# Second-layer weights loaded as two neighbouring rows a partition, weight loads thinned out beside the last attention blocks, and routing placements issued later

## The chip, the cores and the metric

The kernel runs on one core of a Trainium2 chip. The metric is the device time of one execution in microseconds. "TensorE" is PE in the profile, "VectorE" DVE, "ScalarE" ACT, "GpSimd" POOL and "SyncE" SP; PEld is TensorE's weight load. The median of three timed runs before the change is 332.24 us.

## The reference

Retention attention over 8 batches, 8 heads, 576 positions and 64 dimensions a head, then a mixture of 8 experts in which each of the 4608 tokens goes to the one expert with the highest logit.

```python
scores = scale * np.matmul(q, k.transpose(0, 1, 3, 2))
ret = scores * Dmat[None, :, :, :]          # gamma_h ** (i - j), causal
x = np.matmul(ret, v)                       # -> x of 4608 x 512
logits = x @ w_gate
expert_idx = np.argmax(logits, axis=1)
...
for e in range(E):                          # 8 experts
    mask = expert_idx == e
    h = np.maximum(x[mask] @ w1[e], 0.0)    # w1[e]: 512 x 1024
    out[mask] = gate_w[mask, None] * (h @ w2[e])   # w2[e]: 1024 x 512
```

## The kernel before

The order of instructions is written out by hand: each engine executes its instructions in the order in which the program issues them, and waits only on data and on buffers.

**Attention.** `blocks` lists 40 blocks, 5 for each of the 8 batches (four of 128 positions, one of 64). The loop over them overlaps stages of neighbouring blocks: transposes, scores, products with values, states. The kernel writes x, in rows, to a DRAM tile `x_rows`, to which a column block `gat` of gate values is added for each batch (SyncE issues both: `put_rows`, `write_gates`). For each finished batch a chain of small VectorE operations (`route_batch`) works out the slot of each token. It contains two products on TensorE: the ranks (`oh` and `incl` with `su1` and `onesb`) and the placements (`pay` with `rh`); `product` issues the next of the two, `steps` the VectorE operations up to it.

**Experts.** When the first five batches are placed, GpSimd gathers rows of `x_rows` by token number (`gather`, tile `xg`, 128 rows each). Each expert has two items: phase 0 with 3 groups of 128 tokens, phase 1 with 2. The list `seq` begins (0,0), (1,0), (0,1), (1,1), (2,0), (2,1), (3,0) and so on; the first number is the expert. For each item `mm1` makes the hidden layer `ht` from the transposed rows `xt` and the first-layer weights `w1b`; `mm2` multiplies it with the second-layer weights `w2b` in 8 chunks `fb` a group, VectorE scales the result by the gate (`ys`), and GpSimd scatters it to `out`. `trans` transposes the rows of the next item between the groups.

**Queues that matter here.** `load_w` loads one part of an expert's weights: four parts of `w1` (128 rows of 1024 values each) and four of `w2` (two chunks of 128 rows of 512 values). The loads turn float32 into bfloat16 and are issued on GpSimd, in one row with its gathers, scatters and tensor operations. `wq` lists the parts by expert: `w1` parts 0 to 3, then `w2` parts 4 to 7. I number the parts of experts 0 and 1 from 0 to 15, so 12 to 15 are expert 1's `w2`. `fetch(n)` issues the next n parts. The dictionary `early` says how many go beside the last attention blocks; one `fetch` follows after the loop; the rest go out in `on`, which is called after each block of `mm1` (8 calls in phase 0, 4 in phase 1) and after each group of `mm2`. The number n in `on` counts these calls: n = 0 to 7 lie in `mm1(0,0)`, 8 to 10 in `mm2(0,0)`, 11 to 18 in `mm1(1,0)`, and 19 to 21 in `mm2(1,0)`. The `script` names what else is done at given n, among it the last placements (`turn`).

PSUM tiles of `mm1` (`pm`) and of the routing products (`pss`) come in turn from one pool of three banks, `psH`, in this stretch: a new tile waits until the third last one has been read.

Of the kernel before, what the change touches and what calls it, by code (L numbers as in the profile page):

```python
# [19 lines left out]
P = 128  # L20
B, H, S, DH = 8, 8, 576, 64
DM = H * DH
E, F = 8, 1024
# [6 lines left out]
NPT = DM // P  # L30
# [7 lines left out]
EW = 2  # L38
# [6 lines left out]
def kernel(  # L45
# [16 lines left out]
    def mm(out, lhsT, rhs, start, stop):  # L62
        nc.tensor.matmul(out=out, lhsT=lhsT, rhs=rhs, start=start, stop=stop, skip_group_check=True)  # L63
# [44 lines left out]
    NB = len(blocks)  # L108
# [48 lines left out]
    for g in range(2):  # L157
        hs = slice(g * NP, (g + 1) * NP)
        nc.sync.dma_start(out=qts[0][:, hs, 0:NCH - 1, :],
                          in_=q[0, hs, P:NCH * P, :].rearrange("h (p s) d -> p h s d", p=P))  # L160
# [103 lines left out]
    def load_w(e, part, n, pool, dep=None):  # L264

        if part == 0:
            wb[e] = (pool.tile([P, NPT, F], BF16, tag="w1", name="w1b"),
                     pool.tile([P, NFB, DM], BF16, tag="w2", name="w2b"))
        m = (NPT, NFB)[part // n] // n
        o = part % n * m  # L270
        w = (moe_w1, moe_w2)[part // n]
        after(nc.gpsimd.dma_start(out=wb[e][part // n][:, o:o + m, :],  # L272
                                  in_=w[e, o * P:(o + m) * P, :].rearrange("(c p) f -> p c f", p=P)), dep)

# [227 lines left out]
    def stage_R(i):  # L504

        if i < 0:
            return
        b, c = blocks[i]
        full = c < NCH
        n, m = (NP, P) if full else (NP // 2, REM)  # L510
        ps = pools["R"](NP)[0:m]
        xb = xbs.pop(i)


        for k in range(n):
            w, a = k // (n // 2), k % (n // 2)
            for u in range(2):
                r = slice(u * DH, (u + 1) * DH)
                o = (ps[r, 2 * a:2 * a + 2, w * DH:(w + 1) * DH] if full
                     else ps[:, 2 * u + w, :].rearrange("p (h d) -> p h d", d=DH))  # L520
                tr(o, xb[:, k * P + u * DH:k * P + (u + 1) * DH], (identb, identx)[w][:, :])
        xr = wk4.tile([P, NP * P], BF16, tag="xr", name="xr")
        t0 = b * S + c * P
        nc.scalar.copy(out=xr[0:m, :].rearrange("p (a t) -> p a t", t=P), in_=ps)  # L524
        todo_x.append((x_rows[t0:t0 + m, 0:DW], xr[0:m, :].bitcast(F32)))
# [3 lines left out]
    def put_rows():  # L529

        while todo_x:
            o, a = todo_x.pop(0)
            nc.sync.dma_start(out=o, in_=a)
# [15 lines left out]
    def stage_L2(b):  # L549
        ps = small()  # L550
        for h in range(2):
            mm(ps[:, h * 32:h * 32 + (32, E)[h]], lt[:, h * P:(h + 1) * P],
               sel[:, NCH * h:NCH + h, :].rearrange("p c n -> p (c n)"), h == 0, h == 1)
        todo_r.append(route_batch(b, ps[:, 0:NCOL * E].rearrange("p (c n) -> p c n", n=E)))
        for _ in range(2):
            next(todo_r[-1])
# [7 lines left out]
    fields, o = {}, 0  # L564
# [216 lines left out]
    def small():  # L781
        return pools["S"]([P, 512], F32)
# [16 lines left out]
    def mm1(e, ph, between):  # L799
        nb = (CA if ph == 0 else CB) // P  # L800
        n = nb * P
        xt = xts.pop((e, ph))
        w1b, w2b = wb[e]
        ht = (hta if ph == 0 else htb).tile([P, NFB, n], BF16, tag="ht", name="ht")
        per = 512 // n
        for f0 in range(0, NFB, per):
            pm = pools["H"]([P, per, n], F32)
            for o in range(per):
                fb = f0 + o
                for c in range(NPT):  # L810
                    mm(pm[:, o, :], w1b[:, c, fb * P:(fb + 1) * P], xt[:, c, :], c == 0, c == NPT - 1)
            nc.scalar.activation(out=ht[:, f0:f0 + per, :], in_=pm[:, :, :], func=AF.Relu)  # L812
            between()
        return ht
# [43 lines left out]
        return [2 * c - 6, 2 * c - 5] if b == 0 and c > 2 else [c - 1] if b > 0 and c > 0 else []  # L858

    wq = [(e, j) for e in range(EW) for j in range(8)] + [(e, j) for e in range(EW, E) for j in range(8)]  # L860
    early = {NB - 7: 1, NB - 6: 2, NB - 5: 2, NB - 4: 1, NB - 3: 1, NB - 2: 1, NB - 1: 2}

    def fetch(n):
        for e, j in [wq.pop(0) for _ in range(min(n, len(wq)))]:
            load_w(e, j, 4, wpool if e < EW else wpool2)
# [65 lines left out]
        if 0 not in slots and len(placed) == BA and c == NCH:  # L931
            make_slots(0)
    gather_first(len(first))
    fetch(len(wq) - 8 * (E - EW))
    pp.close()
    pq = ExitStack()
    psT = pq.enter_context(tc.tile_pool(name="psT", bufs=2, space=PSUM))
# [14 lines left out]
    def turn():  # L952
        product(rf)
        steps(rf, 9)

    script = {0: lambda: stage_L2(B - 1), 1: turn, 2: lambda: (stage_R(NB - 1), put_rows()), 5: turn,
              9: lambda: (turn(), make_slots(1))}
    calls = iter(range(1000))
    last.append(True)
# [1 line left out]
    def on(i):  # L961

        n = next(calls)
        script.get(n, lambda: None)()
        write_gates()
        gather_upto(i + 2)
        if n > 7 and n * 9 % 20 < 9:
            fetch(1)

    seq = ([(e, 0) for e in range(NA)] + [(e, 1) for e in range(NA)]  # L970
# [71 lines left out]
    with tc.If(over > 0):  # L1042
        with ExitStack() as p3:
# [13 lines left out]
            for f in range(2):  # L1057
                src = ev[:, f, :].rearrange("p (b c) -> p b c", c=NCOL)
                dst = nat[f, :].rearrange("(b s) -> b s", s=S)
                for c in range(NCOL):  # L1060
                    n = P if c < NCH else REM
                    w = nc.sync.dma_start(out=dst[:, c * P:c * P + n].rearrange("b p -> p b"), in_=src[0:n, :, c])
# [18 lines left out]
            xt = fb1.tile([P, NPT, P], BF16, name="fxt")  # L1081
            with tc.For_i(0, nr, 1) as t:
# [7 lines left out]
                with tc.For_i(0, E, 1) as e:  # L1090
# [7 lines left out]
                    for f0 in range(0, NFB, 4):  # L1098
                        pm = fps.tile([P, 4, P], F32, name="fpm")
# [45 lines left out]
```

## Time and profile before

| | us |
|---|---|
| median of 3 runs (331.92, 332.24, 336.05) | 332.24 |
| the profiled execution, its own time | 332.26 |
| its span, first to last instruction | 330.4 |
| time outside the span | 1.9 |
| TensorE busy | 310.5 |
| GpSimd busy | 202.5 |

Attention fills the span to about 170 us, the experts the rest. The last TensorE instruction ends near 325 us, and the last scatter's landing closes the span. Idle time of an engine is of interest only where another engine then waits for it.

### The profile page before, as it was taken

The numbers are of one execution on the slowest core, as the hardware profiler recorded it, in microseconds if no ns is written. First come the engines' busy times: TensorE is split into PE (matmuls) and PEld (weight loads), VectorE is DVE, ScalarE is ACT, GpSimd is POOL, SyncE is SP. The second block draws the span as 40 slices with busy tenths as digits, with TensorE's granted clock in tenths as the row PEclk, the third lists the DMA queues.
The fourth block names the chain that finished last, engine by engine and source line by source line (L and its number), as shares of the span: only waits on it lengthen the run. The fifth ranks groups of instructions, "written<-read, shape, count | busy, mean of one in ns | idle before, by whom it ended". The sixth has DMA issues, their size and how long they took to land. (4 is left out here: it accounts for less than half of the span.)

```text
span 330.4 us, 11777 instructions
## 1 busy us (share of the span) xinstructions
PE 310.5 (94%) x4965; PEld 231.7 (70%) x4981; DVE 135.3 (41%) x412; ACT 184.1 (56%) x372; POOL 202.5 (61%) x259
## 2 busy tenths in 40 slices
PE   7999799999999999997888999999999999989993
PEld 5788689888898888887765556656565655646562
DVE  4434256466565646655357622212122313112122
ACT  3469477676777667675565344554545353554530
POOL 4476654635364452554870488888888788888532
PEclk9999999999999999999999999999999999999998
DMA  9999899999998999899799279989999998999921
GB/s 177 229 250 219 183 238 223 233 229 242 247 225 204 223 219 245 199 192 190 127 225 191 77 141 202 217 198 182 216 198 228 206 223 183 188 227 180 263 96 53
DMA packets 118359, 65.96 MB, mean 200 GB/s; under 512 B 89628, under 2 KB 110620, under 8 KB 118304
## 3 DMA queue, kind: packets, MB, share of 16 engines
q0 software_dynamic: 18432, 31.80, 46.1%
q1 hardware_dynamic: 99344, 33.37, 44.6%
q8 instruction: 40, 0.66, 0.9%
q14 instruction: 15, 0.12, 0.1%
q10 hardware_dynamic: 528, 0.02, 0.1%
HBM read 67.45 MB, written 15.53 MB: 251 GB/s over the span
## 5 line engine op out<-in xcount | busy, mean ns | idle before, releaser
L812 ACT ACTIVATE ht<-pm 128x384 bf16<-128x384 f32 (+1 forms) x96 | 50.4, 525 | 57.4 <-PE pm L63 56.6
L308 POOL TENSOR_TENSOR kk<-kt,kg 128x512 f32<-128x512 f32 x39 | 41.4, 1061 | 65.6 <-issue 36.2
L63 PE MATMUL py<-w2b,ht 128*128 128x512 bf16 (+1 forms) x312 | 73.8, 374 | 2.0 <-DMA w2b<-in_moe_w_dram 1.1
L63 PE MATMUL pm<-xt,w1b 128*128 128x384 bf16 (+1 forms) x512 | 72.8, 299 | 0.0
L1005 DVE TENSOR_SCALAR ys<-py,gsl 128x512 f32<-128x512 f32 (+1 forms) x41 | 30.2, 738 | 85.1 <-PE py L63 81.3
L63 PEld LDWEIGHTS <-w1b 128*128 128x128 bf16 x512 | 49.8, 98 | 21.5
L1008 POOL DMA_INDIRECT out_dram<-ys,tids x40 | 41.2, 1031 | 35.3 <-DVE gsl L796 16.2
L433 DVE TENSOR_TENSOR sc<-pssc,mask 128x512 f32<-128x512 f32 x64 | 41.2, 686 | 28.6 <-PE pssc L63 28.6
L63 PEld LDWEIGHTS <-ht 128*128 128x128 bf16 x328 | 30.8, 98 | 31.1 <-issue 1.4
L752 POOL DMA_INDIRECT xg<-x_rows,tidg x40 | 41.2, 1031 | 14.7 <-issue 8.2
L63 PE MATMUL psx<-sc,vt 128*64 128x128 f32 (+1 forms) x640 | 38.4, 265 | 0.4 <-ACT xT L478 0.3
L63 PE MATMUL pssc<-qT,kT 64*64 64x128 f32 (+2 forms) x896 | 36.6, 262 | 0.1
L478 ACT COPY xT<-psx 128x512 f32<-128x512 f32 x32 | 18.7, 586 | 29.8 <-PE psx L63 21.6
L797 ACT COPY xt<-pt 128x512 bf16<-128x512 bf16 x40 | 22.7, 587 | 18.9 <-PE pt L66 18.8
L298 POOL TENSOR_TENSOR qq<-qt,qg 128x512 f32<-128x512 f32 (+1 forms) x28 | 29.4, 1049 | 6.2 <-DMA qt<-in_q_dram 4.3
L366 ACT COPY kT<-pst 128x512 f32<-128x512 f32 x40 | 23.6, 589 | 17.2 <-PE pst L66 16.3
L63 PEld LDWEIGHTS psx<-sc,vt 128*64 128x64 f32 (+1 forms) x640 | 30.6, 136 | 1.5 <-ACT xT L478 0.4
L63 PEld LDWEIGHTS pssc<-qT,kT 64*64 64x64 f32 (+1 forms) x896 | 29.0, 143 | 2.9 <-ACT qT L351 0.5
L524 ACT COPY xr<-pssc 128x512 bf16<-128x512 bf16 (+1 forms) x38 | 22.6, 594 | 6.5 <-PE pssc L66 6.3
L63 PE MATMUL pss<-vt,kk 128*64 128x64 f32 x512 | 22.5, 230 | 3.0 <-issue 3.0
L272 POOL DMA_DIRECT2D w2b<-in_moe_w_dram x32 | 24.1, 776 | 0.8 <-DMA w1b<-in_moe_w_dram 0.6
L63 PEld LDWEIGHTS pss<-vt,kk 128*64 128x64 f32 x512 | 18.2, 140 | 4.9 <-issue 3.2
(135 smaller groups left out, 374.2 us busy)
## 6 DMA issues: line engine op xcount, KB each, us to landing
kt<-in_k_dram SPq DMA_DIRECT2D x32, 256.0 KB, 5.5
vt<-in_v_dram SPq DMA_DIRECT2D x32, 256.0 KB, 5.0
w1b<-in_moe_w_dram POOLq DMA_DIRECT2D x32, 256.0 KB, 6.0
w2b<-in_moe_w_dram POOLq DMA_DIRECT2D x32, 256.0 KB, 6.8
qt<-in_q_dram SPq DMA_DIRECT2D x14, 512.0 KB, 5.8
x_rows<-xr SPq DMA_DIRECT2D x32, 128.0 KB, 4.9
kt<-in_q_dram SPq DMA_DIRECT2D x8, 128.0 KB, 6.0
kt<-in_k_dram SPq DMA_DIRECT2D x8, 128.0 KB, 5.5
```

The costliest lines, as they stand in the source:

```text
L63: nc.tensor.matmul(out=out, lhsT=lhsT, rhs=rhs, start=start, stop=stop, skip_group_check=True)
L272: after(nc.gpsimd.dma_start(out=wb[e][part // n][:, o:o + m, :], in_=w[e, o * P:(o + m) * P, :].rearrange("(c p) f -> p c f", p=P)), dep)
L298: eng.tensor_tensor(out=qq[:, 0:n, :].rearrange("p s (h d) -> p h s d", d=DH), in0=qts[b][:, h0:h0 + 2, 0:n, :], in1=qg[:, o:o + n, h0:h0 ...
L308: eng.tensor_tensor(out=kk[:, :, :], in0=kts.pop(i)[:, :, :], in1=kg[:, blocks[i][1], :].unsqueeze(2).to_broadcast([P, H, DH]), op=ALU.mult)
L366: mark["kT"] = nc.scalar.copy(out=kT[:, :, :].rearrange("p a (u t) -> p u a t", u=2), in_=ps[:, :, o:o + 256].rearrange("p u (a t) -> p u ...
L433: mark["sc"] = nc.vector.tensor_tensor(out=sc[:, j, :, :], in0=pssc[j][:, :].rearrange("p (a i) -> p a i", i=P), in1=mask[:, :].unsqueeze( ...
L524: nc.scalar.copy(out=xr[0:m, :].rearrange("p (a t) -> p a t", t=P), in_=ps)
L752: nc.gpsimd.indirect_dma_start(out=xg[:, :], out_offset=None, in_=x_rows[0:nr, :], in_offset=bass.IndirectOffsetOnAxis(ap=slots[ph][1][:, ...
L797: nc.scalar.copy(out=xts[(e, ph)][:, :, j * P:(j + 1) * P], in_=pt[:, :, :])
L812: nc.scalar.activation(out=ht[:, f0:f0 + per, :], in_=pm[:, :, :], func=AF.Relu)
L1005: nc.vector.tensor_scalar(out=ys[:, r], in0=py[:, r], scalar1=gsl[:, e, slots[ph][2] + j:slots[ph][2] + j + 1], scalar2=None, op0=ALU.mult)
L1008: scatters.append(nc.gpsimd.indirect_dma_start(out=next(outs)[:, :], out_offset=bass.IndirectOffsetOnAxis(ap=slots[ph][0][:, e, j:j + 1], ...
```

## The change

Four edits. A `w2` part is read from DRAM so that partition p gets the two neighbouring rows 2p and 2p+1 of a block of 256, where it got rows p and p+128. The hidden unit that chunk `fb` holds in partition p changes with it, so `mm1` takes every second column of a block of 256 columns of `w1b`. The tables of `early`, of `fetch` after the loop and of `on` are changed. Two of the three late `turn` calls move, from n = 1 to 3 and from n = 5 to 6.

```diff
@@ load_w
-                                  in_=w[e, o * P:(o + m) * P, :].rearrange("(c p) f -> p c f", p=P)), dep)
+                                  in_=w[e, o * P:(o + m) * P, :].rearrange(
+                                      "(c p) f -> p c f" if part < n else "(p c) f -> p c f", p=P)), dep)
@@ mm1
-                    mm(pm[:, o, :], w1b[:, c, fb * P:(fb + 1) * P], xt[:, c, :], c == 0, c == NPT - 1)
+                    mm(pm[:, o, :], w1b[:, c, fb // 2 * 2 * P + fb % 2:fb // 2 * 2 * P + 2 * P:2], xt[:, c, :],
+                       c == 0, c == NPT - 1)
@@ order of the loads
-    early = {NB - 7: 1, NB - 6: 2, NB - 5: 2, NB - 4: 1, NB - 3: 1, NB - 2: 1, NB - 1: 2}
+    early = {NB - 6: 1, NB - 5: 1, NB - 4: 1, NB - 3: 1, NB - 2: 1, NB - 1: 1}
...
-    fetch(len(wq) - 8 * (E - EW))
+    fetch(4)
...
-    script = {0: lambda: stage_L2(B - 1), 1: turn, 2: lambda: (stage_R(NB - 1), put_rows()), 5: turn,
+    script = {0: lambda: stage_L2(B - 1), 2: lambda: (stage_R(NB - 1), put_rows()), 3: turn, 6: turn,
               9: lambda: (turn(), make_slots(1))}
...
-        if n > 7 and n * 9 % 20 < 9:
+        if n < 4 or n > 7 and n * 11 % 20 < 11:
             fetch(1)
```

In the order of instructions, first GpSimd beside the last attention blocks. In these rows `kk` is attention's scaled keys, `xg` a gather, and each `w1b` or `w2b` row a part of weights. Before:

```order
L308 TENSOR_TENSOR kk<-kt,kg 128x512
L272 DMA w1b<-in_moe_w_dram 128x1024 x2
L308 TENSOR_TENSOR kk<-kt,kg 128x512
L272 DMA w1b<-in_moe_w_dram 128x1024
L272 DMA w2b<-in_moe_w_dram 128x2x512
L308 TENSOR_TENSOR kk<-kt,kg 128x512
L752 DMA xg<-x_rows,tidg_3533 128x272
```

Now:

```order
L309 TENSOR_TENSOR kk<-kt,kg 128x512
L272 DMA w1b<-in_moe_w_dram 128x1024
L309 TENSOR_TENSOR kk<-kt,kg 128x512
L272 DMA w1b<-in_moe_w_dram 128x1024
L309 TENSOR_TENSOR kk<-kt,kg 128x512
L753 DMA xg<-x_rows,tidg_3531 128x272
```

Two parts stand there instead of four, and with the one that stood a little earlier three fewer of the five go out ahead of the first gather; a `w2` part has the shape of a `w1` part.

GpSimd again, where the experts begin; `out_dram` is a scatter, and the three scatters are those of item (0,0). Before:

```order
L272 DMA w1b<-in_moe_w_dram 128x1024 x2
L272 DMA w2b<-in_moe_w_dram 128x2x512 x4
L1008 DMA out_dram<-ys,tids_3532 4608x512 x2
L752 DMA xg<-x_rows,tidg_4190 128x272 x2
L272 DMA w1b<-in_moe_w_dram 128x1024
L1008 DMA out_dram<-ys,tids_3532 4608x512
```

Now:

```order
L272 DMA w2b<-in_moe_w_dram 128x1024 x2
L272 DMA w1b<-in_moe_w_dram 128x1024 x4
L272 DMA w2b<-in_moe_w_dram 128x1024 x2
L1010 DMA out_dram<-ys,tids_3530 4608x512
L272 DMA w2b<-in_moe_w_dram 128x1024
L1010 DMA out_dram<-ys,tids_3530 4608x512
L753 DMA xg<-x_rows,tidg_4189 128x272 x2
L1010 DMA out_dram<-ys,tids_3530 4608x512
L272 DMA w2b<-in_moe_w_dram 128x1024
```

All 16 parts of experts 0 and 1 stood ahead of the first scatter; now 14 do, part 14 follows the first scatter and part 15, the last quarter of expert 1's `w2`, the third.

SyncE, its last writes to `x_rows`, before:

```order
L533 DMA x_rows<-xr 128x256 x2
L727 DMA x_rows<-gat 128x5x16 x2
L533 DMA x_rows<-xr 64x256
L1040 TENSOR_LOAD fi
L1042 COMPARE_AND_BRANCH
```

Now:

```order
L534 DMA x_rows<-xr 128x256 x2
L534 DMA x_rows<-xr 64x256
L728 DMA x_rows<-gat 128x5x16 x2
L1042 TENSOR_LOAD fi
L1044 COMPARE_AND_BRANCH
```

The last 64 rows of x no longer stand behind the two writes of gates. On TensorE only the two routing products move, by two blocks of `mm1` and by one; the order of VectorE's and ScalarE's instructions is the same in both kernels.

## Rows read from the trace of the kernel before

**Rows 1.** The page: the span, TensorE's busy line, and the instruction queue of section 3.

```profile
span 330.4 us, 11777 instructions
...
PE 310.5 (94%) x4965; PEld 231.7 (70%) x4981; DVE 135.3 (41%) x412; ACT 184.1 (56%) x372; POOL 202.5 (61%) x259
...
q8 instruction: 40, 0.66, 0.9%
```

**Rows 2.** Two stretches: length; busy us of PE, PEld, DVE, ACT, POOL; clock; DMA share; GB/s.

```profile
140.00:180.00 40.00, 34.26 (x780) 27.79 (x776) 22.42 (x84) 24.43 (x52) 21.93 (x27) 1.00 0.96 187
180.00:320.00 140.00, 138.09 (x923) 84.94 (x937) 35.99 (x95) 65.98 (x127) 105.30 (x120) 1.00 0.88 188
```

**Rows 3.** TensorE in order of time: start, length, work, idle time before it.

```profile
152.54 0.51 PE L63 MATMUL pss<-vt,kk 128*64 128x64 f32 x10 [1.69 <-issue]
...
158.54 0.27 PE L63 MATMUL pss<-vt,kk 128*64 128x64 f32 x2 [1.30 <-issue]
...
176.66 0.46 PE L63 MATMUL pss<-pay,rh 128*128 128x80 bf16 x5 [1.06 <-DVE pay L701]
...
193.16 1.89 PE L63 MATMUL py<-w2b,ht 128*128 128x512 bf16 x7
```

**Rows 4.** Busy time from the end of the first such wait to that of the second.

```profile
152.54:158.53 5.99, 4.69 (x127) 4.11 (x127) 3.37 (x9) 2.33 (x5) 2.55 (x3) 1.00 0.60 123
```

**Rows 5.** The same view for single microseconds: inside the two waits, and after the last matmul.

```profile
151.00:152.00 1.00, 0.00 (x0) 0.00 (x0) 0.96 (x5) 0.11 (x1) 0.00 (x0) 1.00 1.05 176
...
157.00:158.00 1.00, 0.24 (x9) 0.15 (x4) 1.00 (x3) 0.32 (x1) 0.99 (x1) 1.00 0.06 8
...
328.00:329.00 1.00, 0.00 (x0) 0.00 (x0) 0.00 (x0) 0.00 (x0) 0.00 (x0) 0.72 0.06 21
```

**Rows 6.** VectorE in order of time, the routing chain at the start of the experts.

```profile
176.04 0.56 DVE L701 TENSOR_TENSOR pay<-scr,fld 128x400 bf16<-128x400 f32 x1
...
176.75 0.20 DVE L631 TENSOR_TENSOR d<-pss,mx 128x40 f32<-128x40 f32 x1
```

**Rows 7.** ScalarE in order of time, there.

```profile
176.98 0.24 ACT L633 ACTIVATE ex<-d 128x40 f32<-128x40 f32 x1 [1.81 <-DVE d L631]
177.12 0.47 ACT L812 ACTIVATE ht<-pm 128x384 bf16<-128x384 f32 x1
```

**Rows 8.** GpSimd in order of time: a late weight load, then scatters and gathers.

```profile
150.26 0.72 POOL L272 DMA_DIRECT2D w2b<-in_moe_w_dram  x1
...
185.72 1.08 POOL L1008 DMA_INDIRECT out_dram<-ys,tids  x1 [12.86 <-DVE gsl L796]
...
190.82 0.61 POOL L272 DMA_DIRECT2D w1b<-in_moe_w_dram  x1
191.74 1.03 POOL L1008 DMA_INDIRECT out_dram<-ys,tids  x1 [0.30 <-DVE gsl L796]
```

**Rows 9.** DMA issues from 180 to 196 us: count, size, us to landing.

```profile
w1b<-in_moe_w_dram POOLq DMA_DIRECT2D x2, 256.0 KB, 4.5
```

**Rows 10.** The tile w1b, over the whole span: time from issue to landing.

```profile
DMA to landing us min/median/max: 4.0/6.0/8.3
```

**Rows 11.** GpSimd's groups: count, busy time, mean ns of one, idle before.

```profile
L272 POOL DMA_DIRECT2D w2b<-in_moe_w_dram x32 | 24.1, 776 | 0.8 <-DMA w1b<-in_moe_w_dram 0.6
L272 POOL DMA_DIRECT2D w1b<-in_moe_w_dram x32 | 19.1, 609 | 0.0
```

**Rows 12.** TensorE in order of time, late in the experts.

```profile
261.28 3.66 PE L63 MATMUL pm<-xt,w1b 128*128 128x256 bf16 x32
...
268.90 5.36 PE L63 MATMUL pm<-xt,w1b 128*128 128x384 bf16 x32
...
295.35 0.59 PE L63 MATMUL py<-w2b,ht 128*128 128x512 bf16 x2 [1.12 <-DMA w2b<-in_moe_w_dram]
```

**Rows 13.** Weight loads of TensorE by shape: count, busy time, mean ns.

```profile
L63 PEld LDWEIGHTS <-w1b 128*128 128x128 bf16 x512 | 49.8, 98 | 21.5
```

**Rows 14.** Weight loads in order of time, a run of float32 loads in attention.

```profile
147.84 0.55 PEld L63 LDWEIGHTS pss<-vt,kk 128*64 128x64 f32 x16
```

## The prediction

> **What bounds the kernel now.** I read the stretches first. From 180 to 320 us, the experts, TensorE is busy 138.09 of 140 us at a granted clock of 1.00 [rows 2]; a gain there can only come out of the 1.9 us that are left, or out of shorter matmuls, and the change alters no matmul's size. Of the idle time there one piece is named: 1.12 us in which `mm2` waits for a part of `w2b` [rows 12]. From 140 to 180 us TensorE is idle 40 - 34.26 = 5.7 us [rows 2]. The order of time shows the large pieces of it: 1.69 us and 1.30 us that nothing in the profile explains ("issue"), and 1.06 us in which the placement product waits for VectorE's `pay` [rows 3]. The weight loads begin only at about 141 us, so the change has nothing to act on before that, and the tail after the last matmul is a scatter that it doesn't touch. So everything that can be gained is 5.7 + 1.9 = 7.6 us, and what is named is 1.69 + 1.30 + 1.06 + 1.12 = 5.2 us. Two per cent is 6.6 us; that is also about what a measurement of this kernel tells from no change.
>
> GpSimd is the engine behind it: busy 105.3 of the 140 us [rows 2] with a pause of 0.30 us ahead of nearly each scatter and gather [rows 8]. Whatever is queued on it, in order, sets when weights and rows arrive.
>
> **The change part by part.**
>
> The thinned loads. The two "issue" waits look like waits for instructions. Between the ends of the two lie 127 matmuls and 127 weight loads [rows 4], 254 instructions, and the instruction queue moved 0.66 MB in 40 packets, 16.5 KB each [rows 1]. The first falls right behind a weight issue at 150.26 [rows 8], with the DMA engines full (1.05); in the second they are nearly empty (0.06) [rows 5], so there a single laggard is waited for. The Trainium skill, "Runtime: NRT & Kernel Launch", section Instruction fetch mechanics, says that instructions come in 16 KiB blocks of 256, and that the cost of crossing a block is mostly hidden. The block size agrees with the rows; "hidden" does not fit 1.69 and 1.30 us, and if it held, the waits would have another cause and the gain below would be 0. Three fewer parts go out ahead of the first gather, so the queue in front of the fetch is shorter. Bounds: nothing of the 2.99 us, or all of it. I take half, 1.5, because the first wait stands in full DMA traffic, which the edit thins, and the second in empty engines, where it is not plain what a shorter queue does.
>
> The placements moved. At n = 1 TensorE waited 1.06 us for `pay`, ready at 176.60 [rows 3, 6]. At n = 3 it comes later and finds it ready. But VectorE works `d` right behind `pay`, to 176.95 [rows 6], and two things hang on `d`: the PSUM bank of the logits, which the third next tile of `psH` needs, and ScalarE's `ex`, which held ScalarE 1.81 us and with it the next `ht` to 177.59 [rows 7]. VectorE's and ScalarE's orders are the same, so with the placement gone from n = 1, block 3 of `mm1` waits for that bank until about 177.0, the placement for the bank of block 1 until 177.6, and blocks 4 and 5 for ScalarE. I follow this bank by bank with 0.65 us a block (5.36 / 32 x 4 = 0.67 [rows 12]) and 0.49 us a relu and get the end of `mm1(0,0)` 0.4 us earlier. Bounds: 0 and 1.06; I take 0.4. The rank product then stands some 0.3 us later, and so do VectorE's chain behind it and the first scatter. On SyncE the last x rows move ahead of the gates' writes, which shortens what the next gathers wait for; nothing waits there now, so 0.
>
> The late `w2` wait. The new rule fetches in 11 of 20 calls, where it was 9, so late parts go out earlier: at n = 100 it has issued 14 + 0.55 x 92 = 64, all of them, where 16 + 0.45 x 92 = 57 were out. The 1.12 us [rows 12] go. Bounds 0 and 1.12; I take 1.1, as the parts come whole groups earlier.
>
> GpSimd's issue. A `w2` part takes 776 ns of GpSimd, a `w1` part 609 [rows 11]; in the new form both have one shape, so I take 609 (bounds 609 and 776). One expert takes about 18.4 us of TensorE in steady state (5.36 + 3.66 in `mm1` [rows 12], 40 `mm2` chunks at 1.89 / 8 [rows 3]). GpSimd needs 10 x (1.03 + 0.30) = 13.3 us for its gathers and scatters, and, of 17 calls, 7.65 parts x 0.69 = 5.3 before, 9.35 x 0.61 = 5.7 now: 18.6 before, 19.0 now. It falls behind by half a microsecond an expert, some 3 us by n = 100, and recovers the wait below besides. Cost 0.
>
> Parts 14 and 15. Here the change adds a wait. Before, all of expert 1's `w2` was issued ahead of the first scatter. Now part 15, chunks 6 and 7, stands on GpSimd behind all three scatters of (0,0) and the two gathers of (0,1). Before, GpSimd started these at 185.72 and reached the third scatter at 191.74, without a pause beyond the 0.30, with one `w1` part of 0.61 among them [rows 8]. Now a `w2` part of the same length stands among them instead, so the third scatter starts at 191.74 again, plus the 0.3 of VectorE's delay, and part 15 is issued at 191.74 + 1.03 + 0.3 = 193.1. Two `w1` parts issued there, in quiet traffic, landed after 4.5 us [rows 9]; the shortest of all took 4.0, the median 6.0 [rows 10]. I take 4.5, the same stretch: 197.6. TensorE starts `mm2(1,0)` at 193.16 and needs chunk 6 after six eighths of 1.89 us, 194.6 [rows 3], less the 0.4 gained: 194.2. It waits 3.4 us (2.9 with 4.0, 4.9 with 6.0). Behind it on TensorE is everything else, with nothing to hide it; the fetches and gathers behind part 15 on GpSimd are not delayed by it.
>
> The interleaved columns. 512 weight loads read every second bfloat16. Such a load is not in the trace. A load takes 98 ns [rows 13] beside a matmul of 3.66 / 32 = 114 or 5.36 / 32 = 168 ns [rows 12], so it costs nothing while it takes less than 114. The nearest rows with a step of 4 bytes are float32 loads: 16 of 64 columns over all rows in 0.55 us [rows 14], 69 ns for 128 columns, with the matmuls between them. I take 0; the other end is below. No reason gives a gain.
>
> **The sum.** From the profiled execution's own 332.26 us (span 330.4 [rows 1] and 1.9 around it), which is the median, 332.24: - 1.5 - 0.4 - 1.1 + 3.4 = 332.7 us.
>
> **The rivals.**
>
> Thinning brings nothing, because the waits for instructions fall as they like: 332.26 - 0.4 - 1.1 + 3.4 = 334.2. For it speaks the second wait, in empty DMA engines.
>
> Everything named is gained and part 15 costs its least: 332.26 - 5.2 + 3.3 = 330.4 (TensorE is then 1.06 earlier at chunk 6, 193.5, and with no delay on VectorE and a landing of 4.0 the part is there at 196.8); with a landing a microsecond faster 329.4.
>
> The issue stays at 776 ns: GpSimd then needs 13.3 + 9.35 x 0.69 = 19.8 us an expert, 7 us behind by n = 100, less the 3.4 recovered at part 15 and less about a microsecond of slack of the gathers: some 2 us more, 334.7.
>
> Slower than before, by one mechanism: the strided load. If a step of two elements doubles the load to 196 ns, it passes the matmul, and `mm1` goes by loads: 256 x (196 - 114) + 256 x (196 - 168) = 28 us, 361. It decides from 114 ns on. Against it stand the float32 loads. The Trainium skill, "TensorE: Matmul & The Clock Gate", section Weight-path perf modes, says that the fast load reads 32 bits at a time, two bfloat16; with a step of two, half of each read would be thrown away, which gives this doubling. The same section allows steps, and no run here shows it yet.
>
> The chunk lands late and cold: with 8.3 us [rows 10] the wait is 7.2, and the clock may fall in it (once TensorE was out of work at the end, it was down to a mean of 0.72 between 328 and 329 [rows 5]): 332.26 - 0.4 - 1.1 + 7.2 + 1 or more = 339.
>
> **How the numbers follow.** Forecast 0.50, thinning without effect 0.22, all gains 0.12, issue not cheaper 0.06, strided load 0.05, part 15 late and cold 0.03, unknown gains beyond 6.6 us 0.02. Slower by over 2% is the strided load and the late chunk, 0.08; faster by over 2% needs nearly all idle time there is, 0.02; within 2%, 0.90. The range runs from the full gain with a quick landing, 329.4, to the forecast without thinning at a landing of 6.0 with the late gathers' 1 to 2 us half counted, 336.8.
>
> **What would show it.** Right: a wait of 3 to 4 us in `mm2(1,0)`, six chunks in, for a `w2b` part; GpSimd's `w2b` near 610 ns; no wait near 295; weight loads of `w1b` still near 98 ns; `pay` no longer waited for but short waits for ScalarE or VectorE in `mm1(0,0)`. Wrong: part 15 landing before 195, waits for `xg` late in the experts, `w1b` loads above 114 ns, or waits for instructions at new places between 141 and 180.

## The result, and the profile after

| | us |
|---|---|
| changed kernel, median of 20 runs (330.51 to 336.68) | 333.43 |
| kernel before, median of 20 runs beside it (328.15 to 336.05) | 332.01 |
| ratio, 95% interval | 1.0072, 1.0043 to 1.0101 |
| changed kernel, span of the profiled execution | 331.3 |

The change makes no difference of 2 per cent; if anything it costs 0.7 per cent. The forecast was 332.7 us with a range of 329.4 to 336.8. A ratio here leaves out runs that lie more than 1.5 per cent above the fastest of their kernel, so it is not quite the ratio of the two medians.

The page of the changed kernel, its span, its busy line and the queue of GpSimd's transfers:

```profile
span 331.3 us, 11778 instructions
...
PE 309.8 (94%) x4965; PEld 230.4 (70%) x4981; DVE 136.1 (41%) x412; ACT 184.3 (56%) x372; POOL 195.5 (59%) x259
...
q0 software_dynamic: 14336, 31.80, 43.2%
```

The queue moves 14336 packets where it moved 18432 before, with the same 31.80 MB. GpSimd's busy time fell by 7.0 us (202.5 in [rows 1]), the span grew by 0.9. To see where, I cut both executions at four points that stand in every kernel here: the first product of the gates with x near 133 us (a row of 32 matmuls with `wgp`), the first matmul with `w1b`, the first matmul of `mm1(1,0)`, and the start of the last matmul of `mm2`. I call the stretches A (the last attention blocks and the routing), B (item (0,0)) and C (all other items). The view of stretches, columns as in [rows 2]; first the kernel before:

```profile
133.11:173.77 40.66, 35.98 (x926) 30.90 (x925) 22.14 (x75) 25.33 (x54) 25.06 (x31) 1.00 0.91 185
173.77:187.73 13.96, 12.84 (x91) 7.29 (x90) 10.19 (x42) 6.16 (x13) 1.70 (x2) 1.00 0.71 128
187.73:324.90 137.17, 135.26 (x906) 84.22 (x919) 31.64 (x75) 64.35 (x122) 105.11 (x120) 1.00 0.89 192
```

and the changed kernel:

```profile
133.26:172.17 38.91, 36.37 (x927) 31.11 (x926) 22.67 (x75) 25.42 (x54) 22.46 (x29) 1.00 0.91 190
172.17:185.37 13.20, 12.73 (x91) 7.38 (x91) 10.18 (x42) 5.93 (x13) 1.37 (x2) 1.00 0.66 120
185.37:325.80 140.43, 135.41 (x905) 84.06 (x919) 31.63 (x75) 64.47 (x122) 101.33 (x122) 1.00 0.84 193
```

A gained 40.66 - 38.91 = 1.75 us, B 13.96 - 13.20 = 0.76, C lost 140.43 - 137.17 = 3.26. With 0.15 from the identical code ahead of A (133.26 against 133.11) that is the 0.9 us of the span. TensorE's busy time in C is the same to 0.15 us; what grew is its idle time, 1.91 to 5.02 us.

In A both waits of [rows 3] are gone: the ten matmuls that stood behind the first now stand in one row of 16 with their six neighbours, and the view lists no wait there. One wait of 0.72 us stands earlier, where the kernel before shows none. TensorE in order of time:

```profile
136.71 0.34 PE L66 MATMUL pst<-ident,qq 64*128 64x64 f32 x5 [0.72 <-issue]
...
151.50 0.93 PE L63 MATMUL pss<-vt,kk 128*64 128x64 f32 x16
```

For B and C the same view names what changed:

```profile
175.39 0.82 PE L63 MATMUL pm<-xt,w1b 128*128 128x384 bf16 x4 [0.41 <-DVE d L632]
...
185.37 5.36 PE L63 MATMUL pm<-xt,w1b 128*128 128x384 bf16 x32
...
190.80 1.46 PE L63 MATMUL py<-w2b,ht 128*128 128x512 bf16 x5
194.92 0.59 PE L63 MATMUL py<-w2b,ht 128*128 128x512 bf16 x2 [2.66 <-DMA w2b<-in_moe_w_dram]
...
294.74 0.40 PE L66 MATMUL pt<-identb,xg 128*128 128x128 bf16 x4 [1.57 <-DMA xg<-x_rows,tidg]
```

Two waits make up C's loss: 2.66 us for `w2b`, six chunks into `mm2(1,0)`, and 1.57 us late for a gather. The wait of 1.12 us for `w2b` near 295 [rows 12] is gone, and of the 1.06 us for `pay` [rows 3] a wait of 0.41 for `d` is left. GpSimd in order of time holds the causes of the two new waits:

```profile
184.00 1.04 POOL L1010 DMA_INDIRECT out_dram<-ys,tids  x1 [13.81 <-DVE ys L1007]
...
189.92 1.01 POOL L1010 DMA_INDIRECT out_dram<-ys,tids  x1 [0.30 <-issue]
190.94 0.60 POOL L272 DMA_DIRECT2D w2b<-in_moe_w_dram  x1
...
288.51 1.05 POOL L753 DMA_INDIRECT xg<-x_rows,tidg  x1 [0.30 <-issue]
```

Part 15 goes out at 190.94, right behind the third scatter of (0,0), and is waited for until 194.92. The gather that TensorE misses at 293.2 (294.74 - 1.57) goes out at 288.51; it takes some 6 us to land, where the median of all gathers of this execution is 4.6, so the wait is a late issue and a slow landing together. The issues from 180 to 196 us (count, size, us to landing), which answer to [rows 9]:

```profile
w2b<-in_moe_w_dram POOLq DMA_DIRECT2D x2, 256.0 KB, 3.9
```

GpSimd's groups, answering to [rows 11], and the weight loads of `w1b`, answering to [rows 13]:

```profile
L272 POOL DMA_DIRECT2D w2b<-in_moe_w_dram x32 | 18.5, 586 | 0.7 <-DMA w1b<-in_moe_w_dram 0.4 <-issue 0.2
L272 POOL DMA_DIRECT2D w1b<-in_moe_w_dram x32 | 18.3, 597 | 1.8 <-DMA w2b<-in_moe_w_dram 1.8
...
L63 PEld LDWEIGHTS <-w1b 128*128 128x128 bf16 x512 | 49.9, 98 | 21.9 <-DVE d L632 0.6
```

A `w2` part now costs GpSimd what a `w1` part does, and a strided weight load takes the 98 ns of a contiguous one.

### The profile page after: what moved, and what is told of

The parts are those of the page before. It is cut to its first block, busy times and chain, and to the rows that moved or that the text cites. A ratio compares the mean times of both kernels' runs of the same rounds, so it can differ in the third digit from the quotient of the medians.

```text
span 331.3 us, 11778 instructions
## 1 busy us (share of the span) xinstructions
PE 309.8 (94%) x4965; PEld 230.4 (70%) x4981; DVE 136.1 (41%) x412; ACT 184.3 (56%) x372; POOL 195.5 (59%) x259
## 3 DMA queue, kind: packets, MB, share of 16 engines
q0 software_dynamic: 14336, 31.80, 43.2%
## 5 line engine op out<-in xcount | busy, mean ns | idle before, releaser
L753 POOL DMA_INDIRECT xg<-x_rows,tidg x40 | 41.1, 1028 | 13.1 <-issue 10.0
L63 PE MATMUL pssc<-qT,kT 64*64 64x128 f32 (+2 forms) x896 | 35.8, 259 | 1.0 <-ACT se L411 0.7
L63 PEld LDWEIGHTS pssc<-qT,kT 64*64 64x64 f32 (+1 forms) x896 | 28.2, 140 | 4.0 <-ACT se L411 0.9
L63 PE MATMUL pss<-vt,kk 128*64 128x64 f32 x512 | 21.8, 227 | 0.0
L66 PE MATMUL pst<-ident,kk 64*128 64x64 f32 x320 | 18.7, 234 | 1.8 <-issue 0.7
L289 ACT CAST xb<-xT 128x512 bf16<-128x512 f32 x32 | 20.3, 636 | 0.0
```

The costliest lines, as they stand in the source:

```text
L289: nc.scalar.copy(out=xbs[i][:, :], in_=src)
L753: nc.gpsimd.indirect_dma_start(out=xg[:, :], out_offset=None, in_=x_rows[0:nr, :], in_offset=bass.IndirectOffsetOnAxis(ap=slots[ph][1][:, ...
```

## The experiments

The theory: thinning, the moved placements and the new layout each give time, and two things take it back: part 15 behind the scatters, and GpSimd, which with 11 fetches in 20 calls falls behind, so that late gathers come late. The rivals are that the layout itself costs, that thinning gives nothing and the waits of A wander, and that the gain of a mended kernel belongs to the chip. e1 to e4 ran together on one chip beside the kernel before, and so did e5 to e8, e9 and e10, and e11 and e12; all but e9 and e10 on the same chip.

| kernel | median us | before us | ratio, 95% interval | A | B | C |
|---|---|---|---|---|---|---|
| e1 | 335.27 | 336.7 | 1.0059, 1.0009 to 1.0109 | 44.2 | 13.96 | 135.8 |
| e2 | 340.7 | 336.7 | 1.0182, 1.0119 to 1.0245 | 41.7 | 13.96 | 144.9 |
| e3 | 337.0 | 336.7 | 1.0025, 0.9978 to 1.0072 | 43.2 | 13.20 | 137.9 |
| e4 | 337.67 | 336.7 | 1.0054, 1.0005 to 1.0103 | 39.0 | 13.20 | 141.9 |
| e5 | 331.3 | 336.55 | 0.9868, 0.9803 to 0.9932 | 43.1 | 13.20 | 136.0 |
| e6 | 334.9 | 336.55 | 0.9931, 0.9883 to 0.9978 | 41.1 | 13.96 | 137.0 |
| e7 | 335.26 | 336.55 | 0.9998, 0.9956 to 1.0041 | 41.3 | 13.21 | 141.4 |
| e8 | 338.17 | 336.55 | 1.0049, 0.9978 to 1.0121 | 46.0 | 13.95 | 136.4 |
| e9 | 333.8 | 336.41 | 0.9941, 0.9901 to 0.9982 | 40.8 | 13.20 | 137.1 |
| e10 | 332.52 | 336.41 | 0.9889, 0.9846 to 0.9933 | 38.9 | 13.21 | 135.9 |
| e11 | 335.56 | 334.28 | 1.0034, 0.9984 to 1.0085 | 39.6 | 13.21 | 141.1 |
| e12 | 339.28 | 334.28 | 1.0154, 1.0086 to 1.0222 | 39.6 | 13.20 | 145.8 |

A, B and C are of one profiled execution each. B and C are worth reading to some tenths; A is not: the same program took 43.1 us there in e5 and 38.9 in e10.

**e1, the layout alone.** The kernel before with the edits of `load_w` and `mm1` (lines shortened):

```diff
-  .rearrange("(c p) f -> p c f", p=P)
+  .rearrange("(c p) f -> p c f" if part < n else "(p c) f -> p c f", p=P)
...
-  w1b[:, c, fb * P:(fb + 1) * P]
+  w1b[:, c, fb // 2 * 2 * P + fb % 2:fb // 2 * 2 * P + 2 * P:2]
```

> The kernel before with the new layout alone (w2 rows in pairs, w1 columns interleaved). Theory (the layout's effect is GpSimd time, the strided loads cost nothing): w2b issues fall from 776 to about 590 ns, w1b loads stay at 98 ns, the 1.1 us wait for a w2 part late in the experts goes, the rest stays: 331.0 us against 332.0, ratio 0.995 to 1.000. Rival (a step of two costs TensorE something that the load's length does not show): w1b matmuls further apart, slower than before, ratio above 1.005.

In C no wait of half a microsecond is left and 135.84 us remain, 1.33 less than before:

```profile
190.96:326.80 135.84, 135.05 (x905) 84.19 (x919) 31.55 (x75) 64.44 (x122) 100.39 (x120) 1.00 0.87 194
```

So the late `w2` wait goes with the cheaper issue alone, at 9 fetches in 20, and in this profile the strided columns cost TensorE nothing. The times don't decide: the median lies 1.4 us below that of before, but the ratio lies 0.6 per cent above, with no change just outside its interval, which is the sign that I had given for the rival. Against the rival stand C, where TensorE is busy 135.05 us against 135.26 before, and the kernels e5 and e10 below, which hold the layout and are faster than before. In this profile A holds a wait of 2.16 us for instructions and a fall of the granted clock behind it; the rows are in the last section.

**e2, the loads alone.** The kernel before with the three edits of the loads, the old layout and the old placements:

```diff
-    early = {NB - 7: 1, NB - 6: 2, NB - 5: 2, NB - 4: 1, NB - 3: 1, NB - 2: 1, NB - 1: 2}
+    early = {NB - 6: 1, NB - 5: 1, NB - 4: 1, NB - 3: 1, NB - 2: 1, NB - 1: 1}
...
-    fetch(len(wq) - 8 * (E - EW))
+    fetch(4)
...
-        if n > 7 and n * 9 % 20 < 9:
+        if n < 4 or n > 7 and n * 11 % 20 < 11:
```

> The kernel before with the new order of loads alone, old layout (w2b issues stay at 776 ns). Theory (part 15 late, and GpSimd falls behind with the denser late loads): a wait of 3 to 3.5 us in mm2(1,0), late gathers waited for by 2.5 to 4 us, the waits for instructions between 141 and 180 us gone (-3 at most): 334.5 to 336 us, ratio 1.008 to 1.012, slower than the full change. Rival (the late gather in the trace of the full change was chance): like the full change, 333.4, ratio 1.004.

The time missed the expectation upwards, 1.0182 against 1.008 to 1.012. C takes 144.9 us: 2.5 us for part 15, 2.2 us for gathers, and waits for ScalarE's `ht` and `xt`, the largest 1.57. One of the gather waits, in TensorE's order of time:

```profile
299.07 0.40 PE L66 MATMUL pt<-identb,xg 128*128 128x128 bf16 x4 [1.61 <-DMA xg<-x_rows,tidg]
```

The late wait of 1.12 us for `w2b` [rows 12] is gone here too, at the old price of the issue. The edits of the loads are the part of the change that costs; with the old, dearer issue on GpSimd they cost 144.9 - 140.4 = 4.5 us more in C than with the new one.

**e3, the placements alone.**

```diff
-    script = {0: lambda: stage_L2(B - 1), 1: turn, 2: lambda: (stage_R(NB - 1), put_rows()), 5: turn,
+    script = {0: lambda: stage_L2(B - 1), 2: lambda: (stage_R(NB - 1), put_rows()), 3: turn, 6: turn,
```

> The kernel before with the two placements moved alone. Theory (most of the wait for VectorE is only handed on to banks and ScalarE): mm1(0,0) takes 0.4 to 0.8 us less from its first matmul to its last, a wait of 0.4 us behind VectorE's d stays: 331.5, ratio 0.998. Rival (the whole wait of 1.06 us is gained): 330.9, ratio 0.9965, no wait in mm1(0,0).

B falls from 13.96 to 13.20 us, exactly as in the changed kernel. That is 0.2 per cent, which the times can't show (1.0025, with no change inside the interval); the late `w2` wait stands in C again, with 1.11 us.

**e4, all 16 parts ahead of the experts' first scatters.** The changed kernel with

```diff
-    fetch(4)
+    fetch(6)
```

> The full change, but with six parts instead of four after the loop, so that all 16 parts of experts 0 and 1 go out ahead of the first scatter. Theory (part 15's place is what the change loses, but its wait also let GpSimd catch up): the 2.7 us wait in mm2(1,0) is gone, GpSimd has two parts fewer later (1.2 us) but 2.7 us less to recover in, so the late gathers are waited for by 2 to 4 us: 331.5 to 332.5, ratio 0.999 to 1.001. Rival (GpSimd is not behind; the late gather was chance): the whole wait is gained, 330.7 or less, ratio 0.996 or less. Third (the wait in mm2(1,0) only hid another one right behind it): no faster than the full change, 333.4.

The time is 1.0054, not the 0.999 to 1.001 that I expected; the third guess, no faster than the full change, is what came. The wait for part 15 is gone, and C is 1.5 us longer for all that, 141.9. In its place, in TensorE's order of time:

```profile
210.04 0.75 PE L66 MATMUL pt<-identb,xg 128*128 128x128 bf16 x8 [0.57 <-DMA xg<-x_rows,tidg]
...
295.87 0.40 PE L66 MATMUL pt<-identb,xg 128*128 128x128 bf16 x4 [1.23 <-DMA xg<-x_rows,tidg]
...
301.40 1.89 PE L63 MATMUL py<-w2b,ht 128*128 128x512 bf16 x8 [1.45 <-DVE gsl L797]
```

With two more gather waits of 0.41 and 0.44 that is 4.1 us (`gsl` is read from gathered rows, so its wait is one for a gather too). The gather of the row at 295.87 is the 34th, as is that of the changed kernel's late wait. GpSimd in order of time:

```profile
290.25 1.05 POOL L753 DMA_INDIRECT xg<-x_rows,tidg  x1 [0.30 <-issue]
```

That is 102.8 us behind the start of C (290.25 - 187.41); in the changed kernel it was 103.1 (288.51 - 185.37). In the changed kernel GpSimd does 27 scatters, 27 gathers and 48 weight loads in those 103.1 us, and its pauses beyond the usual 0.30 come to 2.7 us. So GpSimd keeps its own pace, whether TensorE waits for part 15 or not: with that wait TensorE is held back with it, without it TensorE stands for the gathers. So mending one of the two losses gains nothing.

**e5, both losses mended.** e4 with

```diff
-        if n < 4 or n > 7 and n * 11 % 20 < 11:
+        if n < 4 or n > 7 and n * 9 % 20 < 9:
```

> The full change, with six parts after the loop (all 16 parts of experts 0 and 1 ahead of the first scatter) and the late loads at 9 of 20 calls as before. Theory (GpSimd's queue decides both losses): neither a wait for w2b in mm2(1,0) nor late gathers; from the first matmul of mm1(1,0) to the last group of mm2 135.8 to 136.3 us as with the layout alone, mm1(0,0) 13.2 us, the end of attention as in the full change: ratio 0.985 to 0.992 to the kernel before. Rival (the denser late loads are not what delays the gathers; removing part 15's wait only moves it): waits for gathers of 2 us or more remain, ratio 0.997 or more.

No wait of half a microsecond is left in C (136.0 us), and the kernel is 1.3 per cent faster than before, although its A holds a wait of 1.89 us and a fall of the clock. This version beats both kernels, the changed one on the same chip (335.56 in e11).

**e6, thinning alone.** The kernel before with the new `early` of e2 and no other edit.

> The kernel before with the thinner loads beside the last attention blocks alone (6 parts instead of 10; the other ten of experts 0 and 1 at once after the loop). Theory (fewer loads shorten the waits for instructions): from the gate product of the sixth batch, near 133 us, to the first matmul with w1b 39 to 41 us, where kernels with ten parts took 40.7, 44.2 and 43.2; ratio 0.990 to 0.996. Rival (these waits wander from run to run and have nothing to do with the loads): 41 to 44 us, ratio 0.998 to 1.003.

The ratio is 0.9931, with no change outside the interval; B and C are those of before (13.96, and 137.0 with the late `w2` wait at 0.98). Of the waits for instructions in A the first of [rows 3] is down from 1.69 to 0.79, the second, 1.30, is gone, and 0.72 stand at 138.18, where the kernel before shows none. The first, in TensorE's order of time:

```profile
154.22 0.51 PE L63 MATMUL pss<-vt,kk 128*64 128x64 f32 x10 [0.79 <-issue]
```

But A as a whole is 41.1 us, no shorter than the 40.66 before and within what the rival expects, since TensorE is busy 37.23 us in it where it was 35.98. So the time speaks for thinning, with about 0.7 per cent (0.2 to 1.2) or 2.3 us, and this profile shows shorter waits but no shorter stretch.

**e7, the slower pace from n = 12 on.** The changed kernel, with parts 14 and 15 where it has them:

```diff
-        if n < 4 or n > 7 and n * 11 % 20 < 11:
+        if n < 4 or n > 7 and (n * 11 % 20 < 11 if n < 12 else n * 9 % 20 < 9):
```

> The full change with its late loads at 9 of 20 calls from n = 12 on, part 15 where the change has it. Theory: the wait for w2b in mm2(1,0) stays, 2.5 to 3.5 us, the late gathers are not waited for, 138.5 to 139.5 us from the first matmul of mm1(1,0) to the last group of mm2; ratio 0.993 to 1.000. Rival (the denser loads are not the cause): waits for gathers of 1.5 us or more remain, 140.4 us or more.

No gather is waited for late, as the theory has it, and the ratio, 0.9998, lies at the end of its range, but C takes 141.4 us where it expects 138.5 to 139.5. TensorE's order of time, and one microsecond in the view of stretches behind it:

```profile
195.65 0.69 PE L63 MATMUL py<-w2b,ht 128*128 128x512 bf16 x2 [2.79 <-DMA w2b<-in_moe_w_dram]
```

```profile
196.00:197.00 1.00, 1.00 (x8) 0.59 (x6) 0.62 (x1) 0.20 (x1) 1.00 (x3) 0.50 0.98 103
```

The wait for part 15 drew a fall of the granted clock to half behind it, which I had not expected. So this wait can cost more than its length.

**e8, more loads in A.** The kernel before with all 16 parts beside the last eight blocks:

```diff
-    early = {NB - 7: 1, NB - 6: 2, NB - 5: 2, NB - 4: 1, NB - 3: 1, NB - 2: 1, NB - 1: 2}
+    early = {NB - i: 2 for i in range(1, 9)}
```

> The kernel before with all 16 parts of experts 0 and 1 beside the last eight blocks, two each, none after the loop: the opposite of thinning. Theory: more and longer waits for instructions between the gate product near 133 us and the first matmul with w1b, 43 to 47 us there; ratio 1.005 to 1.02. Rival (no connection): 40.5 to 44 us as in the kernel before, ratio 0.998 to 1.003.

A grows to 46.0 us. It holds two waits for instructions at the places where the other kernels have theirs, 1.00 and 2.98, with a fall of the clock behind the second. Two more that the profile leaves unexplained, 0.49 at 174.90 and 1.55 at 177.19, are none of these: they stand where the kernel before waits 0.31 and 0.35 us for ScalarE, and each ends just behind ScalarE's `xb` (174.84) and `xr` (177.13), with no instruction packet ending in the 3 us before. The longest, in TensorE's order of time:

```profile
155.10 0.53 PE L63 MATMUL pss<-vt,kk 128*64 128x64 f32 x10 [2.98 <-issue]
```

Six, ten and sixteen parts beside the last blocks thus give ratios of 0.9931 (e6), 1 (before) and 1.0049 (e8) on one chip. Only the first step is clear of no change (e8: 0.9978 to 1.0121), but both go the same way.

**e9, four parts beside attention.** e5 with

```diff
-    early = {NB - 6: 1, NB - 5: 1, NB - 4: 1, NB - 3: 1, NB - 2: 1, NB - 1: 1}
+    early = {NB - 4: 1, NB - 3: 1, NB - 2: 1, NB - 1: 1}
...
-    fetch(6)
+    fetch(8)
```

> The kernel of the fifth experiment with still fewer loads beside attention: one part beside each of the last four blocks only, eight after the loop. Theory (the loads of blocks NB-6 and NB-5 lengthen the wait for instructions near 151 us): from the gate product near 133 us to the first w1b matmul 38.5 to 40.5 us, no wait over 1.5 us there, the later stages as in the fifth (13.2 and 136 us): ratio 0.980 to 0.988 to the kernel before. Rival (two parts make no difference any more): as the fifth, 0.987, with a stretch of 40 to 43 us.

It missed: 0.9941, no better than e5, and 1.3 us slower than e10 beside it by the medians, though the intervals of the two ratios overlap. A is 40.8 us, though the wait ahead of the row of ten is down to 0.24; 1.27 us stand elsewhere, at 136.56. C has two gather waits, 0.57 and 0.30, in `mm2(1,0)`, behind a pause of 1.97 us on GpSimd. So this one try with fewer than six parts brought nothing more.

**e10, e5 once more.**

> The kernel of the fifth experiment once more, beside the one that thins further, to see how far its stretches repeat. Theory: the later stages repeat within 0.3 us (13.2 and 136), the stretch from 133 us to the first w1b matmul within 2 us (41 to 45 before this look gave 43.1): ratio 0.983 to 0.991. Rival (its gain was the chip's scatter): ratio 0.995 or more.

0.9889 on another chip than e5's 0.9868. C repeats within 0.2 us, B within 0.1; A, 38.9 us against 43.1, does not repeat within the 2 us that I expected. Its three stretches, the view of stretches again:

```profile
136.89:175.82 38.93, 36.93 (x926) 31.31 (x925) 22.73 (x75) 25.11 (x54) 23.48 (x31) 1.00 0.91 186
175.82:189.03 13.21, 12.74 (x92) 7.38 (x91) 10.19 (x42) 5.94 (x13) 1.06 (x2) 1.00 0.81 145
189.03:324.90 135.87, 135.08 (x906) 84.23 (x919) 31.45 (x75) 64.45 (x122) 100.80 (x120) 1.00 0.87 195
```

Against the changed kernel A and B are the same and C is 4.56 us shorter: all of part 15's 2.66 and of the gather's 1.57. GpSimd's 34th gather, in order of time:

```profile
285.77 1.05 POOL L753 DMA_INDIRECT xg<-x_rows,tidg  x1 [0.30 <-issue]
```

It goes out 96.7 us behind the start of C (285.77 - 189.03), 6.4 us earlier than at 11 fetches in 20: from the start of C on, 39 weight loads stand ahead of it on GpSimd, where in the changed kernel there are 48.

**e11, the changed kernel again, and e12, its pace at 9 in 20.** e11 has no edit. e12 is the changed kernel with

```diff
-        if n < 4 or n > 7 and n * 11 % 20 < 11:
+        if n < 4 or n > 7 and n * 9 % 20 < 9:
```

> The changed kernel itself, beside e12 and a kernel before on the same chip as e5 and e10, where its time has not been taken yet. Theory (part 15 behind the scatters and a GpSimd that falls behind eat what the other edits give): ratio to the kernel before 1.000 to 1.010, and 1.1 to 2.0 per cent above e5 and e10 (331.3 and 332.5 us), 335 to 338 us; the trace with 2.5 to 2.9 us for w2b in mm2(1,0) and 1 to 2 us for xg late. Rival (the gain of e5 is this chip's, and the change itself would show it there): ratio 0.985 to 0.993, and then neither fetch(6) nor the pace explains anything.

> The changed kernel with its steady fetching at 9 in 20 calls in place of 11, part 15 left behind the scatters: the price of part 15 by itself, with a GpSimd that keeps up. Theory: the wait of 2.5 to 2.9 us in mm2(1,0) stays, no gather is waited for late in the experts, from the first matmul of mm1(1,0) to the last chunk 136.0 + 2.7 = 138.7 us (a microsecond or two more where the granted clock falls in the wait), and the time lies 0.5 to 0.9 per cent above e5 and e10 and below e11 by 0.3 per cent or more. Rival: with two parts fewer ahead of the experts than e5 the slower pace runs late, and a late w2b wait of 1 us or more comes back near 295 us, as in the kernel before, so that the time equals e11's.

e11 lies where the theory has it: 1.0034, which is 1.7 and 1.5 per cent above the ratios of e5 and e10 (by the medians, 335.56 us, 1.3 and 0.9). It ran on e5's chip, so the gain of e5 is not that chip's. The wait for part 15 is 2.68 us; the late gather's is 0.55, less than expected. TensorE in order of time, and a microsecond behind the first wait in the view of stretches:

```profile
194.74 1.01 PE L63 MATMUL py<-w2b,ht 128*128 128x512 bf16 x2 [2.68 <-DMA w2b<-in_moe_w_dram]
...
295.10 0.40 PE L66 MATMUL pt<-identb,xg 128*128 128x128 bf16 x4 [0.55 <-DMA xg<-x_rows,tidg]
```

```profile
196.00:197.00 1.00, 1.00 (x5) 0.41 (x4) 0.60 (x2) 0.59 (x1) 0.37 (x2) 0.50 0.84 131
```

e12 missed by both expectations, 1.0154. TensorE in order of time:

```profile
193.94 0.86 PE L63 MATMUL py<-w2b,ht 128*128 128x512 bf16 x2 [2.49 <-DMA w2b<-in_moe_w_dram]
198.27 1.01 PE L63 MATMUL py<-w2b,ht 128*128 128x512 bf16 x2 [3.47 <-DMA w2b<-in_moe_w_dram]
...
300.52 0.59 PE L63 MATMUL py<-w2b,ht 128*128 128x512 bf16 x2 [1.18 <-DMA w2b<-in_moe_w_dram]
```

and GpSimd:

```profile
189.11 0.61 POOL L272 DMA_DIRECT2D w2b<-in_moe_w_dram  x1
...
193.73 0.61 POOL L272 DMA_DIRECT2D w2b<-in_moe_w_dram  x1
```

I had overlooked that the rule picks calls as well as a rate: at 11 in 20 the calls n = 8 and n = 10 fetch parts 14 and 15; at 9 in 20 it is n = 9 and n = 12. Both parts stand later among the scatters and gathers, 189.11 and 193.73, and both are waited for, 2.49 and 3.47 us, with the clock near half from 194 to 201. The rival's late `w2b` wait came too, 1.18 and another of 0.59. So it is not a clean test of part 15's price; it shows that at 9 in 20 from n = 8 on, with parts 14 and 15 left among the scatters, the kernel is slower than the changed one.

## Why the prediction held, and which step failed

The time held, and the mechanism of the main term, part 15, but not every term, and the range did part of the work: the gathers' 1.57 us, which had been set at 0, was nearly made up by three other terms that came out 0.25, 0.36 and 0.74 us better than forecast. That these cancel is luck. Of the signs that the prediction gives for being wrong, two came: gathers waited for late in the experts, and part 15 landing before 195, at 194.8. The second says less, as `mm1(1,0)` began 2.4 us earlier than before (185.37 against 187.73); but the wait is 2.66 us, not the 3 to 4 of the sign for being right. By its steps:

**Thinned loads, -1.5.** The profile gives -1.75 in A, but one profile of A proves little: with six parts it took 38.9 to 43.1 us over nine executions (after, e2, e4 to e7, e10 to e12), with ten parts 40.7, 44.2 and 43.2; the three of 43 us and more (e1, e3, e5) hold a fall of the clock. The better evidence is e6's timing, about 2.3 us (0.7 to 3.9), against the rival that thinning brings nothing; e8's points the same way without being clear of noise. Of the path, that the loads delay the fetch of instructions, the traces show one half, which I had overlooked: the waits end with the arrival of instructions. Each of the two waits of [rows 3], and each at their places and at the one near 136 us in the other kernels, ends 1.3 to 1.5 us behind the end of a packet of the instruction queue, `q8`, 16384 bytes each (before: packets from 150.13 to 151.09 and from 156.33 to 157.27, waits to 152.54 and 158.54; e8: 152.68 to 153.64, wait to 155.10). The one behind the first wait is the 27th of 40 packets in every kernel here; in e10, which has no such wait, it ends at 152.71, 1.5 us ahead of the row of matmuls at 154.20. The waits also keep their places: where a kernel shows one near 136 us and one near 152, 379 or 380 matmuls and as many weight loads lie between them, three times some 253 instructions, and from there to the one near 158 it is 127 and 127 (before, e7, e12), 254. That the loads are what makes the packets late stays argued. For it speaks that the first of the two waits of [rows 3] recurs ahead of the same row of ten matmuls with `vt` and `kk`: 0.24 us with four parts (e9); with six none in three profiles and 0.50 to 1.89 in six; 1.69 to 2.25 with ten; 2.98 with sixteen. The Trainium skill, "Runtime: NRT & Kernel Launch", section Instruction fetch mechanics, has the cost of a block's crossing mostly hidden; its block size agrees with these distances, "hidden" does not agree with the 2.98 us in e8.

**Placements, -0.4.** B gave 0.76, in every kernel with the edit. The wait for a bank that `d` still held came, with 0.41 us, so the mechanism was right and the term too small.

**The late `w2` wait, -1.1.** It went, but the faster pace is not the only reason, and not always needed: e1 loses the wait by the cheaper issue at the old pace, e2 by the faster pace at the old issue (with TensorE held back by other waits, too). In the changed kernel with the old pace (e12), which also issues parts 14 and 15 later, it came back with 1.18 us.

**GpSimd, 0.** This step failed. I had GpSimd 19.0 us an expert against TensorE's 18.4, had it fall 3 us behind, and then set the cost at 0, on the ground that the wait for part 15 would let it recover. The cost is 1.57 us in the profile and 0.55 in e11, and 4.1 us once e4 takes away the wait that hides it. The sum that made GpSimd the slower engine was right: 103.1 us for 54 gathers and scatters, ten of which make an expert, are 19.1 us an expert. To write 0 behind it was not: at 19.1 against 18.4 us it does not recover, it is only matched by TensorE's own waits. The issue itself came at 586 ns, a little below the 609 that I took, which was also the lower bound.

**Part 15, +3.4.** 2.66 us in the profile, 2.68 in e11, 2.79 in e7. The order on GpSimd was as read: behind the third scatter. The part landed in 3.9 us where I took 4.5, the [rows 9] price of a `w1` part; the rest is that it went out 1.3 us ahead of the need (190.94 against 194.92 - 2.66 = 192.26) where I had 1.1. The bound of 2.9, from the shortest landing of [rows 10], was thus missed by 0.2. The clock, which fell to half behind this wait in e7, e11 and e12, stood only in a rival and not in the term.

**Strided columns, 0.** 98 ns before and after, and e1's C without a loss. The doubling to 196 ns that I had drawn from the 32-bit reads of the Trainium skill, "TensorE: Matmul & The Clock Gate", section Weight-path perf modes, did not come; that this section allows steps agrees with the 98 ns.

By the profile the sum is 0.15 - 1.75 - 0.76 + 3.26 = +0.9 us against +0.4 predicted. The timed difference is larger in the first comparison, 0.72 per cent or 2.4 us (1.4 to 3.4), and 1.1 in e11 (no change inside its interval). The forecast of +0.4 us thus lies below the interval of the first comparison and within that of e11. A clock that falls in part of the executions would widen the difference: in e11, with a fall, C less its two waits is 141.07 - 2.68 - 0.55 = 137.8 us, in the profile after 140.43 - 2.66 - 1.57 = 136.2. How often the clock falls, in either kernel, was not measured, so this stays open.

## What to carry to other kernels

Add up, per round of the steady state, what the issuing engine needs and what the busiest one needs; where the first is larger, the lag will be paid somewhere, and only waits elsewhere hide it. When a load is moved behind other work in an in-order queue, find the one transfer that is needed first and look at the exact call that issues it: one part behind three scatters instead of ahead of them cost 2.7 us here, about what the thinning of the traffic gave. A loss that is hidden behind another is mended only together with it (e4 gave nothing, e5 and e10 1.1 to 1.3 per cent).

## What the hardware showed that I had not expected

The granted clock fell to half, 1.2 of 2.4 GHz, for some 3 to 4 us behind single waits of TensorE of 1.89 to 2.98 us, with the engine busy before and after. In e1 the wait of 2.16 us ended at 153.43:

```profile
153.43 0.53 PE L63 MATMUL pss<-vt,kk 128*64 128x64 f32 x10 [2.16 <-issue]
```

```profile
154.00:155.00 1.00, 1.00 (x16) 1.00 (x14) 0.26 (x1) 0.57 (x2) 0.90 (x1) 0.50 1.19 242
155.00:156.00 1.00, 1.00 (x11) 0.69 (x7) 0.00 (x0) 0.59 (x3) 0.14 (x1) 0.50 1.12 236
```

In the two rows the clock, the last figure but two, reads 0.50. The same followed waits of 1.89 (e5), 2.25 (e3), 2.98 (e8), 2.79 (e7) and 2.68 us (e11). It did not follow the 2.66 us of the changed kernel's first profile, though that is the same program as e11; there the clock read 1.00 right behind the wait:

```profile
196.00:197.00 1.00, 1.00 (x6) 0.49 (x5) 0.36 (x2) 0.35 (x1) 0.70 (x2) 1.00 1.03 158
```

Nor did it follow the 2.49 us of e2, or the 1.69 us of the kernel before [rows 3]. So such a wait costs its length, or its length and by these two executions of one program some 1.6 us more (137.8 against 136.2 us of C without its waits), and which of the two is not told by its length.
